# A fused backward pass of attention and FFN: when row layouts are staged, how many buffers two tiles have, and where the attention output is copied

## The chip, the cores and the metric

The kernel runs on one core of a Trainium2 chip. The core has a matmul engine (TensorE, PE in the profile; PEld is its weight load), VectorE (DVE), ScalarE (ACT), GpSimd (POOL) and SyncE (SP). Each takes its instructions in the order in which they were written. SP and POOL serve here mostly as queues that issue DMA transfers: an instruction that waits holds up everything behind it on that queue. The metric is the time of one execution on the device in microseconds.

## The reference

With x of 2048 rows of 448 numbers (16 heads of 28), the forward pass is a layer norm followed by an attention block and a gated FFN in parallel, and a residual:

```python
xn = layernorm(x)
q, k, v = split(xn @ wqkv)                  # 16 heads of 28
o = softmax(q @ k.T * 28 ** -0.5) @ v
out = x + o @ wo + (silu(xn @ w_gate) * (xn @ w_up)) @ w_down      # F = 1792
```

The kernel returns `out` and, for a given gradient of `out`, the gradients of x, wqkv, wo, w_gate, w_up and w_down: seven outputs in bf16.

## The kernel before

The work comes in four parts: a prologue (layer norm, transposed copies, the first group's projections), the forward loop, the backward loop over attention, and a last part that assembles the gradient of x. The change touches the forward loop alone.

The forward loop has 256 steps `(g, qc, kt)`: four groups `g` of four heads, four blocks `qc` of 512 queries, sixteen blocks `kt` of 128 keys. In a step PE makes the scores of four heads (L600) into two PSUM tiles `s_ps` of two heads each, of which there are two in all. ACT takes the exponential of each (L605) into a tile `eT`. PE then multiplies the exponentials of the step before with v (`pv`, L582) into the output tile `o_ps`, of which there is one. After the last key block, `pv` calls `o_items`: ACT copies `o_ps` to `o_raw` (L470), and two jobs are put in a queue: `tr`, four transposes of `o_raw` on PE (L479), and `do`, the projected gradient (L501). Their results are normalised on DVE, transposed by SP (L492, L523) and stored.

What is left of a step is filled with other matmuls by `fill(pace)`, which takes jobs from `queue` until the step's share of the remaining cost is used. `push(..., front=True)` puts jobs at the head; `behind=1` leaves the job that is first there in front of them. `cur` holds the rest of the job that is under way, and always comes first. The queue holds:

- the FFN, in 14 chunks `fc` of 128 columns and four row blocks `sc`. Each block makes three products in PSUM tiles `f_ps` (three in all, L383), from which DVE makes the three results in one tile `fT` (L407 and L417). SP transposes `fT` into `f_sp` (L419) and POOL stores it as three pieces of `hd_d` (L422).
- the weight gradients of the chunk before (L357), which need its `f_sp`: 16 matmuls for each of three weights, which take row blocks 0 to 3 in turn. The first weight's matmuls come in row block 1 of the next chunk.
- after a chunk, `weight_layout`: SP transposes a piece of a weight into the buffer `sp_stage` (L300), and POOL stores it (L302).
- at `qc == 2`, the next group's projections (L180), and `proj_done`, which stores them.
- `sp_layouts`, for the backward loop: it brings q and k of a group into row layout. SP transposes qT into `sp_stage` (L211), POOL stores it (L212), then the same for kT. There is one `sp_stage`, which `weight_layout` uses too. The job costs 0 in the planner and is pushed to the head of the queue at `kt == 0` of `qc == 1`. In that same step `pv` finishes block 0 of the queries, so `o_items` pushes its jobs behind the one job at the head, which then is `sp_layouts`.

Of the kernel before, what the change touches and what calls it, by code (L numbers as in the profile page):

```python
# [13 lines left out]
BF16 = mybir.dt.bfloat16  # L14
# [10 lines left out]
P = 128  # L25
NT = S // P
# [11 lines left out]
def kernel(  # L38
# [19 lines left out]
    pe, act, dve, pool, sp = nc.tensor, nc.scalar, nc.vector, nc.gpsimd, nc.sync  # L58
# [11 lines left out]
    spq_d = dram.tile([G, P, NT * P], BF16, name="spq_d")  # L70
    spk_d = dram.tile([G, P, NT * P], BF16, name="spk_d")
# [25 lines left out]
    bst = ExitStack()  # L97
# [6 lines left out]
    wq_sb = w_buf[:].rearrange("p a b -> p (a b)")[:, :4 * 3 * G * P].rearrange(  # L104
        "p (c t g r) -> p c t g r", c=4, t=3, g=G)
    stg = bst.enter_context(tc.tile_pool(name="stg", bufs=1))
    ep = bst.enter_context(tc.tile_pool(name="ep", bufs=7))
    ps_s = bst.enter_context(tc.tile_pool(name="ps_s", bufs=2, space=PSUM))
    ps_o = bst.enter_context(tc.tile_pool(name="ps_o", bufs=1, space=PSUM))
    ps_f = bst.enter_context(tc.tile_pool(name="ps_f", bufs=3, space=PSUM))  # L110
# [17 lines left out]
    for b in (2, 3):  # L128
# [10 lines left out]
        out=r_ones[:], in_=ident_f[:].rearrange("p (a b) -> p a b", b=HP)[:, :, 28:30],  # L139
# [29 lines left out]
    qk_tiles = {}  # L169
# [35 lines left out]
        pool.dma_start(out=qT_d[g], in_=qT[:])  # L205
        pool.dma_start(out=kT_d[g], in_=kT[:])

    def sp_layouts(g):
        for tq, dst in ((0, spq_d), (1, spk_d)):
            s_ = stg.tile([P, NT, P], BF16, name="sp_stage")  # L210
            sp.dma_start_transpose(out=s_[:], in_=qk_tiles[(g, tq)][:])  # L211
            pool.dma_start(out=dst[g], in_=s_[:].rearrange("p t c -> p (t c)"))  # L212

    def ln_stats(b):
        for t in range(4 * b, 4 * b + 4):
# [71 lines left out]

    fst = ExitStack()
    ftmp = fst.enter_context(tc.tile_pool(name="ftmp", bufs=2))
    fT = fst.enter_context(tc.tile_pool(name="fT", bufs=3))  # L290
    spp = fst.enter_context(tc.tile_pool(name="spp", bufs=2))
    op_ = fst.enter_context(tc.tile_pool(name="op_", bufs=1))
    def weight_layout(c, i):
# [15 lines left out]
    def fill(budget):  # L309

        while budget > 0.05:
            if not cur:
                if not queue:
                    return
                cur.extend(queue.popleft())
            cost, fn = cur.popleft()
            fn()
            budget -= cost
            left[0] -= cost

    def push(jobs, front=False, behind=0):
        left[0] += sum(c for job in jobs for c, _ in job)
        if front:
            first = [queue.popleft() for _ in range(min(behind, len(queue)))]
            queue.extendleft(reversed(first + jobs))
        else:
            queue.extend(jobs)

    def proj_items(g):
        out = []  # L330
        for tq in range(3):
            for sc in range(4):
                box = {}

                def go(c, tq=tq, sc=sc, box=box):
                    if c == 0:
                        box["m"] = proj_unit(g, tq, sc, "dve")
                    box["m"](c)
                out.append([(MM, lambda c=c, go=go: go(c)) for c in range(4)])
        out.append([(0.0, lambda: proj_done(g))])  # L340
        return out
# [204 lines left out]
    def load_pair(pr, parts):  # L546

        g, r = pr // 2, 64 * (pr % 2)
        q = qkp.tile([P, S], BF16, name="qT")
        k = qkp.tile([P, S], BF16, name="kT")  # L550
        qd[pr] = (q, k)
        n = S // parts
        return [lambda i=i, dst=dst, r0=r0, src=src: sp.dma_start(
                    out=dst[r0:r0 + 64, i:i + n], in_=src[g, r:r + 64, i:i + n])
                for r0, srcs in ((0, (qT_d, kT_d)), (64, (dOT_d, vT_d)))
                for dst, src in zip((q, k), srcs) for i in range(0, S, n)]

    def load_group(g, parts, kpool):

        spt[g] = [qkp.tile([P, NT, P], BF16, name="v_sp"), kpool.tile([P, S], BF16, name="vT"),  # L560
                  qkp.tile([P, NT, P], BF16, name="O_sp")]
        spt[g][1] = spt[g][1][:].rearrange("p (t c) -> p t c", c=P)
        n = NT // parts
        return [lambda i=i, t=t, src=src: sp.dma_start(
                    out=t[:, i:i + n, :].rearrange("p t c -> p (t c)"), in_=src[g, :, i * P:(i + n) * P])
                for t, src in zip(spt[g], (spq_d, spk_d, spo_d)) for i in range(0, NT, n)]
# [8 lines left out]
    def pv(i):  # L575
        g, qc, kt = steps[i]
        if kt == 0:
            o_cur["o"] = ps_o.tile([P, 512], FP32, name="o_ps")
        o_ps, v = o_cur["o"], v_tiles[g]
        e = eTs.pop(i)  # L580
        for hh in range(4):
            pe.matmul(o_ps[HP * hh:HP * (hh + 1), :], lhsT=v[:, kt, HP * hh:HP * (hh + 1)],  # L582
                      rhs=e[hh // 2][:, hh % 2, :], start=(kt == 0), stop=(kt == NT - 1),
                      tile_position=(0, HP * hh), skip_group_check=True)
        if kt == NT - 1:
            o_items(g, qc, o_ps)

    for i, (g, qc, kt) in enumerate(steps):
        if kt == 0 and qc == 1:
            push([[(0.0, lambda g=g: sp_layouts(g))]], front=True)  # L590
        if kt == 0 and qc == 2 and g + 1 < G:
            push(proj_items(g + 1), front=True)
        qT, kT = qk_tiles[(g, 0)], qk_tiles[(g, 1)]
        pace = left[0] / (nst - i)
        eTs[i] = []
        pair = [ps_s.tile([P, 2, 512], FP32, name="s_ps") for _ in range(2)]
        for half, s_ps in enumerate(pair):
            for j in range(2):
                r = HP * (2 * half + j)
                pe.matmul(s_ps[:, j, :], lhsT=kT[r:r + HP, kt * P:(kt + 1) * P],  # L600
                          rhs=qT[r:r + HP, qc * 512:(qc + 1) * 512],
                          start=True, stop=True, tile_position=(r, 0))
        for s_ps in pair:
            e = ep.tile([P, 2, 512], BF16, name="eT")
            act.activation(out=e[:], in_=s_ps[:], func=ACT.Exp, scale=SCALE)  # L605
            eTs[i].append(e)
        if i >= 1:
            pv(i - 1)
        if g == G - 1 and qc == 2:
            if kt == 0:  # L610
                first = load_pair(0, 1) + load_group(0, 1, vp)
            elif kt % 2 and first:
                first.pop(0)()
        if i in (6, 8, 10, 12):
            j = i // 2 - 3
            sp.dma_start_transpose(out=woT[:, :, j * P:(j + 1) * P], in_=wo_pad[:, j, :])
        pv_next[0] = i
        fill(pace)
# [212 lines left out]
    for k in range(N + 2 * UW):  # L831
        W, pos = k // UW, k % UW
        if k < N:
# [16 lines left out]
            s_ps = ps_sd.tile([P, 2, 512], FP32, name="sd")  # L850
# [25 lines left out]
        if 1 <= k <= N:  # L876
# [5 lines left out]
            if qi not in TQ:  # L882
                sp.dma_start_transpose(out=dsT[:, :, :, qi * P:(qi + 1) * P].rearrange("p j c q -> p (j c) q"),
                                       in_=DS[k - 1][:].rearrange("p j c -> p (j c)"))
# [128 lines left out]
```

## Time and profile before

| | us |
|---|---|
| median of 3 runs (1550.44 to 1550.81) | 1550.76 |
| the profiled execution | 1549.43 |
| its span, first to last instruction | 1547.7 |
| forward loop, about 30 to 656 | 626 |
| backward loop, about 656 to 1490 | 834 |
| last part, from 1490 | 58 |

The mean granted clock of PE over the profiled execution is 0.978 of full speed.

A row of the order of time gives start, duration, engine, line, operation, and in brackets how long the engine stood idle before it and what ended that. "SPq" and "POOLq" are the engines' DMA queues; the duration of a DMA row is the time that issuing took, not that to its landing. A row of the waits gives the sum, the number and the longest. Since busy time is an average over parts with different limits, a change in the forward loop is read from that loop's rows.

### The profile page before, as it was taken

To read this page: it belongs to the slowest core of one execution; us is meant where nothing else is said; L and a number is where in the kernel's file an instruction comes from. 1 tells how busy PE (TensorE), PEld (TensorE's weight loads), DVE (VectorE), ACT (ScalarE), POOL (GpSimd) and SP (SyncE) were. 2 spreads that over 40 slices of the span, in tenths; PEclk is the share of its full clock that TensorE was granted. 3 is DMA by queue.
4 is the path that set the end of the run, shared out by engine and by line. 5 is a ranking of instruction groups with operands and counts; after the bars stand their busy time and mean duration, and the time that the engine had idled before them with its cause. 6 is when DMAs were issued, how large, how long until landed. Compare 5 with 4: busy or idle time off the path is not lost.

```text
span 1547.7 us, 32024 instructions
## 1 busy us (share of the span) xinstructions
PE 1412.8 (91%) x12176; PEld 597.7 (39%) x12176; DVE 1099.4 (71%) x1421; ACT 1187.9 (77%) x1333; POOL 396.1 (26%) x664
## 2 busy tenths in 40 slices
PE   6899999999999989988988988989999889999987
PEld 3333333333333333433433444433335333543353
DVE  7654555656666657476877877878878789888935
ACT  6898988888788878676767867878778778888724
POOL 4341433343435355310110111111102101111033
PEclk9999999999999999999999999999999999999999
DMA  9985758767978689799999999999999999999994
GB/s 225 189 174 113 157 101 173 161 142 141 179 154 164 148 173 215 159 205 200 214 204 206 196 199 205 198 200 198 207 197 197 200 192 197 174 192 215 188 274 142
DMA packets 682106, 285.12 MB, mean 184 GB/s; under 512 B 637136, under 2 KB 650464, under 8 KB 681952
## 3 DMA queue, kind: packets, MB, share of 16 engines
q1 hardware_dynamic: 652016, 210.03, 74.6%
q0 software_dynamic: 25968, 64.53, 16.8%
q10 hardware_dynamic: 3968, 8.52, 1.6%
q8 instruction: 95, 1.56, 0.4%
q14 instruction: 59, 0.48, 0.1%
HBM read 67.34 MB, written 63.44 MB: 85 GB/s over the span
## 4 chain that ended last, share of the span: by engine, by line
PE 56%; DMA 13%; ACT 13%; DVE 8%; issue 6%; SPq 1%; POOL 1%; ACTq 0%; DVEq 0%; POOLq 0%
DMA dsT<-ds 9%; PE f_ps L357 7%; PE sd L852 6%; PE s_ps L600 6%; PE f_ps L383 6%; ACT E L870 5%; PE aux L719 4%; PE acc L749 4%; PE aux L796 4%; PE aux L776 4%; PE o_ps L582 4%; ACT eT L605 4%; DVE ds L881 3%; ACT dsT L783 3%; PE aux L713 3%
## 5 line engine op out<-in xcount | busy, mean ns | idle before, releaser
L881 DVE TENSOR_TENSOR ds<-sd,E 128x1024 bf16<-128x1024 f32 x512 | 611.4, 1220 | 137.5 <-DMA dsT<-ds 52.6
L870 ACT ACTIVATE E<-sd 128x1024 bf16<-128x1024 f32 x512 | 516.9, 1024 | 178.4 <-PE sd L863 140.2
L605 ACT ACTIVATE eT<-s_ps 128x1024 bf16<-128x1024 f32 x512 | 495.8, 1026 | 93.1 <-PE s_ps L600 89.6
L852 PE MATMUL sd<-kT,qT 32*128 32x512 bf16 x1024 | 201.8, 390 | 24.7 <-DVE ds L881 22.3
L863 PE MATMUL sd<-kT,qT 32*128 32x512 bf16 x1024 | 202.6, 389 | 23.6 <-ACT E L870 22.7
L749 PE MATMUL acc<-ds,v_sp 128*32 128x512 bf16 x1024 | 204.6, 395 | 0.7 <-DVE ds L881 0.7
L749 PE MATMUL acc<-E,O_sp 128*32 128x512 bf16 x1024 | 204.3, 395 | 0.2 <-ACT dkv_o L755 0.2
L600 PE MATMUL s_ps<-qT,kT 32*128 32x512 bf16 x1024 | 148.0, 386 | 7.8 <-ACT eT L605 5.6
L422 POOL DMA_DIRECT2D hd_d<-fT x168 | 126.9, 769 | 15.5 <-DVE fT L407 6.8
L383 PE MATMUL f_ps<-xnT,wgu 128*128 128x512 bf16 x448 | 118.8, 383 | 4.9 <-DVE w_sb L409 4.7
L764 POOL DMA_DIRECT2D dqkv_d<-dkv_o x64 | 39.3, 619 | 289.1 <-ACT dkv_o L755 287.3
L719 PE MATMUL aux<-W,ck 128*128 128x448 bf16 x448 | 108.4, 359 | 3.4
L852 PEld LDWEIGHTS <-qT 32*128 32x128 bf16 x1024 | 51.3, 91 | 154.1 <-issue 145.5
L582 PE MATMUL o_ps<-eT,v_sp 128*32 128x512 bf16 x1024 | 103.4, 394 | 0.6
L357 PE MATMUL f_ps<-xn_sp,f_sp 128*128 128x448 bf16 x448 | 99.1, 354 | 0.0
L749 PEld LDWEIGHTS <-O_sp 128*32 128x32 bf16 x1024 | 50.4, 94 | 113.4 <-issue 103.4
L600 PEld LDWEIGHTS <-kT 32*128 32x128 bf16 x1024 | 40.7, 91 | 137.7 <-issue 132.7
L776 PE MATMUL aux<-ident_bf,ds 128*128 128x128 bf16 x1024 | 79.4, 221 | 11.2 <-DVE dq_acc L808 5.8
L863 PEld LDWEIGHTS <-qT 32*128 32x128 bf16 x1024 | 65.4, 91 | 62.1 <-issue 58.2
L357 PEld LDWEIGHTS <-f_sp 128*128 128x128 bf16 x672 | 58.2, 98 | 77.4 <-issue 23.4
L776 PEld LDWEIGHTS <-ds 128*128 128x128 bf16 x1024 | 61.8, 98 | 39.8 <-issue 39.4
L395 DVE SCALAR_TENSOR_TENSOR g<-t_sb,f_ps 128x512 f32<-128x512 f32 x56 | 38.4, 686 | 53.3 <-ACT t_sb L393 53.2
(133 smaller groups left out, 1766.5 us busy)
## 6 DMA issues: line engine op xcount, KB each, us to landing
hd_d<-fT POOLq DMA_DIRECT2D x168, 128.0 KB, 4.4
ck<-hd_d SPq DMA_DIRECT2D x32, 448.0 KB, 4.4
ck<-hd_d SPq DMA_DIRECT2D x16, 576.0 KB, 5.1
dsT<-ds SPq DMA_TRANSPOSE x384, 4.2
dqkv_d<-dkv_o POOLq DMA_DIRECT2D x64, 64.0 KB, 3.8
dq_c<-dqkv_d ACTq DMA_DIRECT2D x5, 768.0 KB, 6.5
W<-wT_d SPq DMA_DIRECT2D x14, 224.0 KB, 3.6
out_dram<-dw_o POOLq DMA_DIRECT2D x28, 96.0 KB, 4.0
```

What stands on the lines that cost most here:

```text
L357: pe.matmul(acc[:, :D], lhsT=src[:, 12 * (t // 4) + 4 * wi + t % 4, :], rhs=rhs[:, t, :D], start=(t == 0), stop=(t == NT - 1))
L383: pe.matmul(st[name][:], lhsT=w(c), rhs=src[:, tsl, c, :], start=(c == 0), stop=(c == 3))
L582: pe.matmul(o_ps[HP * hh:HP * (hh + 1), :], lhsT=v[:, kt, HP * hh:HP * (hh + 1)], rhs=e[hh // 2][:, hh % 2, :], start=(kt == 0), stop=(kt ...
L600: pe.matmul(s_ps[:, j, :], lhsT=kT[r:r + HP, kt * P:(kt + 1) * P], rhs=qT[r:r + HP, qc * 512:(qc + 1) * 512], start=True, stop=True, tile_ ...
L605: act.activation(out=e[:], in_=s_ps[:], func=ACT.Exp, scale=SCALE)
L719: return [lambda n=n: pe.matmul(ps[:, :D], lhsT=t[:, n, :], rhs=w[:, n, :], start=(n == 0), stop=(n == NFC - 1)) for n in range(NFC)]
L749: pe.matmul(acc[r:r + HP, :], lhsT=src[:, qt, 64 * hp + HP * j:64 * hp + HP * j + HP], rhs=m[:, j, :], start=(qt == 0), stop=(qt == NT - 1 ...
L776: pe.transpose(ps[:, i, :], ds[:, i // 4, (i % 4) * P:(i % 4 + 1) * P], ident_bf[:])
L852: pe.matmul(s_ps[:, j, :], lhsT=q[HP * j:HP * j + HP, qt * P:(qt + 1) * P], rhs=kv[HP * j:HP * j + HP, kc * 512:(kc + 1) * 512], start=Tru ...
L863: pe.matmul(d_ps[:, j, :], lhsT=q[r:r + HP, qt * P:(qt + 1) * P], rhs=kv[r:r + HP, kc * 512:(kc + 1) * 512], start=True, stop=True, tile_p ...
L870: act.activation(out=E[k][:], in_=s_ps[:], func=ACT.Exp, scale=SCALE)
L881: dve.tensor_tensor(out=DS[k - 1][:], in0=d_ps[:], in1=E[k - 1][:], op=ALU.mult)
```

## The change

Four edits:

1. `sp_layouts(g)`, which staged q and k one behind the other, becomes `sp_layout(g, tq)`, which stages one of them. q is staged in block 1 of the queries and k in block 2, each at `kt == 4` where both were at `kt == 0` of block 1. Both go to the head of the queue, as before.
2. `fT` has 4 buffers in place of 3.
3. `eT` has 5 buffers in place of 7.
4. `pv(i - 1)` is called after the first of a step's two exponentials, not after the second. PE's order within the step stays; what moves is the copy of `o_ps` to `o_raw` on ACT, which now stands between the two exponentials.

With `sp_layouts` gone from `kt == 0`, the job left in front of `tr` and `do` in block 1 is a job of the FFN, as it is in the other blocks (or one of the next group's projections). All other instructions are the same in number and kind; fillers move by a few places in the forward loop, and the backward loop's order is unchanged.

```diff
-    ep = bst.enter_context(tc.tile_pool(name="ep", bufs=7))
+    ep = bst.enter_context(tc.tile_pool(name="ep", bufs=5))
...
-    def sp_layouts(g):
-        for tq, dst in ((0, spq_d), (1, spk_d)):
-            s_ = stg.tile([P, NT, P], BF16, name="sp_stage")
-            sp.dma_start_transpose(out=s_[:], in_=qk_tiles[(g, tq)][:])
-            pool.dma_start(out=dst[g], in_=s_[:].rearrange("p t c -> p (t c)"))
+    def sp_layout(g, tq):
+        s_ = stg.tile([P, NT, P], BF16, name="sp_stage")
+        sp.dma_start_transpose(out=s_[:], in_=qk_tiles[(g, tq)][:])
+        pool.dma_start(out=(spq_d, spk_d)[tq][g], in_=s_[:].rearrange("p t c -> p (t c)"))
...
-    fT = fst.enter_context(tc.tile_pool(name="fT", bufs=3))
+    fT = fst.enter_context(tc.tile_pool(name="fT", bufs=4))
...
-        if kt == 0 and qc == 1:
-            push([[(0.0, lambda g=g: sp_layouts(g))]], front=True)
+        if kt == 4 and qc in (1, 2):
+            push([[(0.0, lambda g=g, qc=qc: sp_layout(g, qc - 1))]], front=True)
...
-        for s_ps in pair:
+        for half, s_ps in enumerate(pair):
             e = ep.tile([P, 2, 512], BF16, name="eT")
             act.activation(out=e[:], in_=s_ps[:], func=ACT.Exp, scale=SCALE)
             eTs[i].append(e)
-        if i >= 1:
-            pv(i - 1)
+            if half == 0 and i >= 1:
+                pv(i - 1)
```

## The prediction

> **What bounds the kernel now.** I read the page's head first, then busy time by stretch, then who waits for whom in the stretch that the change touches, then the order of time around the longest waits.
>
> ```profile
> span 1547.7 us, 32024 instructions
> ## 1 busy us (share of the span) xinstructions
> PE 1412.8 (91%) x12176; PEld 597.7 (39%) x12176; DVE 1099.4 (71%) x1421; ACT 1187.9 (77%) x1333; POOL 396.1 (26%) x664
> ```
>
> All edits lie in the forward loop of 256 steps, some 626 us long. Its stretch (length, then busy time of PE, PEld, DVE, ACT and POOL, then the granted clock):
>
> ```profile
> 30.00:656.00 626.00, 591.55 (x3924) 223.69 (x3923) 367.14 (x636) 527.45 (x584) 251.39 (x365) 0.98 0.79 160
> ```
>
> The matmul engine is the bound here: 591.55 of 626 us. ACT is second, with 527.45. So work that the change moves costs nothing in itself; what counts is PE's idle 34.5 us and the time that PE runs at a lower clock. The idle time, by who ended it (total, times, longest):
>
> ```profile
> PE f_ps L479 <- ACT o_raw L470: 8.8, 8, 1.8
> PE f_ps L357 <- DMA f_sp<-fT: 8.1, 2, 7.0
> PE s_ps L600 <- ACT eT L605: 5.6, 19, 0.5
> PE f_ps L383 <- DVE w_sb L409: 4.7, 5, 2.5
> PE f_ps L180 <- DVE w_sb L409: 2.2, 1, 2.2
> ```
>
> And four stretches of low clock, each right behind a wait of this list (the third number from the right is the granted clock):
>
> ```profile
> 70.00:76.00 6.00, 5.78 (x38) 3.06 (x39) 2.80 (x6) 3.21 (x5) 0.00 (x0) 0.50 0.98 145
> 216.00:219.00 3.00, 3.00 (x23) 1.87 (x24) 2.01 (x5) 1.04 (x2) 0.88 (x2) 0.51 1.30 96
> 404.00:407.00 3.00, 3.00 (x13) 0.64 (x12) 2.93 (x5) 0.68 (x1) 2.53 (x4) 0.50 1.31 154
> 546.00:550.00 4.00, 3.65 (x15) 1.06 (x16) 0.62 (x1) 1.71 (x2) 1.88 (x3) 0.50 1.01 232
> ```
>
> At half clock, half of PE's busy time is lost: 2.9, 1.5, 1.5 and 1.8 us.
>
> **Staging q and k apart (part A).** Before, both transposes go into one buffer, one behind the other, so k's waits until q has landed and been stored. Both stand on SP's queue ahead of everything else. The fourth group, in order of time:
>
> ```profile
> 525.71 1.72 SPq L211 DMA_TRANSPOSE sp_stage<-qT  x1
> 533.56 3.11 SPq L211 DMA_TRANSPOSE sp_stage<-kT  x1
> 536.77 1.22 SPq L492 DMA_TRANSPOSE oT<-O_sp  x1
> 539.31 0.36 SPq L494 DMA_DIRECT2D hd_d<-oT  x1
> 539.77 1.82 SPq L523 DMA_TRANSPOSE dOT<-dOl  x1
> 541.67 1.57 SPq L419 DMA_TRANSPOSE f_sp<-fT  x1
> ```
>
> The FFN result that the last row transposes was complete on DVE by 531.0 (second row below starts at 530.33 and takes 0.68). It left 10.7 us later, and PE stood until 546.35:
>
> ```profile
> 530.33 0.68 DVE L417 SCALAR_TENSOR_TENSOR fT<-f_ps,w_sb 128x512 bf16<-128x512 f32 x1
> ...
> 546.35 1.30 PE L357 MATMUL f_ps<-dy_sp,f_sp 128*128 128x448 bf16 x3 [7.05 <-DMA f_sp<-fT]
> ```
>
> After the change, in the order of SP's queue, this transpose (that of the last of a chunk's four query blocks, the one that PE needs soonest) stands ahead of the output's transpose, and q's staging comes one FFN block later. It could leave at 531 and land about 4.8 us later (the median row in the last fence), at 536; PE asked for it at 539.3 (546.35 less 7.05). So the wait goes whole, with its dip: 7.05 + 1.8 = 8.85 us. The transposes and the stores, four of each for q and for k, stay in number and size. POOL's stores wait as before for the transpose, but never for two in a row.
>
> What is late next? Each of the eight stagings can still find the buffer taken, by a weight layout, and hold SP meanwhile. The queue's waits of before show the prices:
>
> ```profile
> SPq L211 <- DMA spq_d<-sp_stage: 14.7, 4, 4.3
> SPq L211 <- DMA sp_stage<-qT: 10.1, 4, 2.9
> SPq L211 <- DMA wqT_d<-sp_stage: 9.1, 2, 4.7
> ```
>
> The first two rows, 6.2 us for each group, vanish. The third can come back: in the fourth group's new order a weight layout, 5.4 us in its store (last fence), stands ahead of q's staging with only three transposes between. Behind that staging waits the FFN transpose of the second query block, which PE wants only in the next chunk, about 40 us later (14 chunks in 626 us), and the fourth buffer below gives DVE room. By this the cost is nothing; at the other end it is a hit like the old one, 8.85. I take half a hit, 4.4, since one of eight stagings stands this way.
>
> **Four buffers of FFN results (part B).** With three, DVE waits until an old result has been stored:
>
> ```profile
> DVE fT L407 <- DMA hd_d<-fT: 10.4, 3, 6.2
> ```
>
> While it waits, the third FFN accumulator stays taken, and PE stops for it: the two longest waits on `w_sb` in the list, 2.5 and 2.2, follow the two long ones of DVE. With one buffer more, DVE waits for a store one query block older, and such blocks are some 11 us apart (626 us over 56), more than the 6.2. So 2.5 + 2.2 + 1.5 of dip = 6.2 us; nothing at the worst, if POOL's queue is what is late.
>
> **Five buffers of exponentials.** A step writes two, and the output matmuls of step i-1 stand ahead of the scores of step i+1 in PE's order, so no more than four are alive. Cost nothing; if PE fell behind, ACT would have no scores to work on either.
>
> **The output's transposes in the second query block (part C).** Before, the staging job sat at the head of the queue of fillers and took the place of the one job that should lie between the copy of the output and its transposes. PE ran into the copy:
>
> ```profile
> 70.22 1.12 PE L479 MATMUL f_ps<-ident_f,o_raw 128*128 128x128 f32 x4 [1.75 <-ACT o_raw L470]
> ...
> 215.88 1.01 PE L479 MATMUL f_ps<-ident_f,o_raw 128*128 128x128 f32 x4 [1.76 <-ACT o_raw L470]
> ...
> 524.78 0.66 PE L479 MATMUL f_ps<-ident_f,o_raw 128*128 128x128 f32 x4 [1.05 <-ACT o_raw L470]
> ...
> 651.14 0.66 PE L479 MATMUL f_ps<-ident_f,o_raw 128*128 128x128 f32 x4 [0.68 <-ACT o_raw L470]
> ```
>
> The staging now enters at the fifth step of a block, so an FFN job of four matmuls or more lies between. The first three waits go, with the dips at 70 and 216: 1.75 + 1.76 + 1.05 + 2.9 + 1.5 = 9.0 us. The last one, behind the loop, stays.
>
> The row of low clock stands first: 0.50 begins behind waits of 1.75 and 1.76 us. The Trainium skill, "TensorE: Matmul & The Clock Gate", section "What's actually happening", says that the clock halves after an idle window of about 3.4 us. By that rule waits of 1.75 or 2.5 us would cause no dip, and 5.9 us of the sum would stay; that is the second rival.
>
> **The copy between two exponentials (part D).** The other four waits of the first row, 8.8 - 4.56 - 0.68 = 3.6 us, go too, for the copy ends one exponential (about 1 us) sooner. In exchange the second exponential ends a copy later, and PE's second pair of scores of the next step needs its place. Timing, from a block's end:
>
> ```profile
> 521.82 0.72 PE L600 MATMUL s_ps<-qT,kT 32*128 32x512 bf16 x4
> 522.15 0.09 PEld L600 LDWEIGHTS <-kT 32*128 32x128 bf16 x1 [0.23 <-issue]
> 522.31 1.94 ACT L605 ACTIVATE eT<-s_ps 128x1024 bf16<-128x1024 f32 x2 [0.21 <-PE s_ps L600]
> ...
> 524.14 0.59 ACT L470 COPY o_raw<-o_ps 128x512 f32<-128x512 f32 x1
> ```
>
> Exponentials start 0.49 us after the step's scores; with the copy between, the second ends at 0.49 + 1.94 + 0.59 = 3.0. A step takes 626 / 256 = 2.45 us, less the stalls about 2.4, and its second pair of scores is due 0.33 later, at 2.7. So PE waits 0.3 us, 15 times: 4.5. Bounds: nothing, if a long filler covers it, and a whole exponential, 0.97, each time (14.6). ACT itself does not wait for the output matmuls: they run during the first exponential. Net: 4.5 - 3.6 = 0.9 lost.
>
> ```profile
> wT_d<-sp_stage POOLq DMA_DIRECT2D x6, 448.0 KB, 5.4
> f_sp<-fT SPq DMA_TRANSPOSE x56, 4.8
> ```
>
> **Sum.** -8.85 - 6.2 - 9.0 + 0.9 + 4.4 = -18.7 us. The profiled execution took 1549.43 us, of which 1547.7 are the span; that is 1.3 below the median of the runs, 1550.76. So 1530.7 by the profile, 1532 as a median. The backward loop keeps its order of instructions and starts earlier.
>
> **The rivals.** First: the fourth FFN buffer does not do what it says. If POOL stores late because it stands behind waits for transposes, DVE merely waits one block later. For it: the stores share POOL's queue with every wait named above; against it: only three of 56 results waited. 6.2 us stay: 1538.
>
> Second: the dips do not hang on the short waits. Against it, a dip follows 1.75 and 1.76; for it, no dip follows the 2.2. Then 2.9 + 1.5 + 1.5 stay, and only the 7 us wait's dip goes: 1538. The Trainium skill's rule on the clock gate, above, would lead here.
>
> Third: the copy delays PE by a whole exponential, so 0.97 and not 0.3 for each of 15: 10 us more, 1542. For it, ACT is busy 84% of the loop; against it, waits of PE on exponentials were 0.5 at most.
>
> Fourth, the other side: a staging that finds its buffer taken by a weight layout's store holds back the FFN transpose that PE needs next, at 8.85 us each. There are now eight such places, not four. Parts A to D give 23; from three such hits on (26.6) the kernel is slower, 1554 with three. For it, the two waits of 4.7 and less on `wqT_d`; against it, in the new queue order each staging lies behind the last block's transpose, or long ahead of it.
>
> **How the numbers follow.** Forecast 0.50 (1525 to 1541 on its own), first rival 0.10, second 0.10, third 0.13, fourth 0.13, and 0.04 that losses of several kinds eat the gain. About 0.2%, 3.1 us, can be told from no change. Faster: 0.50 + 0.10 + 0.10 + 0.11 of the third; slower: the fourth and 0.01; same: the rest. The low end is all gains without costs, 8.85 + 6.2 + 9.0 + 3.6 = 27.7 below: 1523. The high end, 1549, leaves out the fourth rival.
>
> **What would show it.** In the profile after: no wait of 7 us for `f_sp`; the staging's wait for its own store gone from SP's queue; DVE no longer waiting for `hd_d`; PE's wait for `o_raw` at about 1 us in total and that for the exponentials up by some 4; no half clock at 70 and 216; the loop near 607 us. I am wrong if a new long wait for `f_sp` stands behind a staging, or if the dips move to other places.

## The result, and the profile after

The changed kernel takes 1534.68 us (median of 5 runs, 1531.74 to 1537.83) against 1550.44 of the kernel before in the same comparison: a ratio of 0.9897, with a 95% interval of 0.9878 to 0.9915. Forecast were 1532 and a range of 1523 to 1549. Line numbers of the changed kernel are one lower from L210 on; in the experiments `a_stage` and `a_split` number their lines like it, `u_stage`, `a_exp`, `a_late`, `a_ffn` and `a_copy` like the kernel before.

The profiled execution of the changed kernel took 1534.68 us. Its head, and then the first matmul of the backward loop by its line (the number ahead of "to" is the start of the first, so the end of the forward loop; in the kernel before it is 656.4):

```profile
span 1532.9 us, 32019 instructions
```
```profile
L851 PE MATMUL sd<-kT,qT x1024: 371/385/605, 643.3 to 1453.2; 32*128 32x512 bf16 x171
```

So 13.1 of the 14.8 us of difference between the two spans lie in the forward loop; the rest takes 891.3 us before and 889.6 after. Who ended PE's waits in the loop after the change:

```profile
PE f_ps L356 <- DMA f_sp<-fT: 8.8, 3, 5.0
PE s_ps L599 <- ACT eT L604: 7.9, 26, 0.6
PE f_ps L382 <- DVE w_sb L408: 1.5, 2, 1.2
...
PE f_ps L478 <- ACT o_raw L469: 0.7, 1, 0.7
```

Two rows shrank: the wait for the output's copy from 8.8 to 0.7 us, and that for `w_sb` from 6.9 to 1.5. The row for exponentials rose by 2.3. The row for `f_sp` did not shrink at all. The 7 us wait of the fourth group is gone, as SP's queue there shows in order of time:

```profile
516.49 1.42 SPq L418 DMA_TRANSPOSE f_sp<-fT  x1
517.99 1.56 SPq L491 DMA_TRANSPOSE oT<-O_sp  x1
523.18 0.36 SPq L493 DMA_DIRECT2D hd_d<-oT  x1
523.64 1.76 SPq L522 DMA_TRANSPOSE dOT<-dOl  x1
525.49 1.26 SPq L299 DMA_TRANSPOSE sp_stage<-in_B_w_gate_dram  x1
526.84 1.21 SPq L163 DMA_TRANSPOSE wdT<-in_B_w_down_dram  x1
528.13 1.18 SPq L164 DMA_TRANSPOSE wdT<-wd  x1
529.41 1.46 SPq L418 DMA_TRANSPOSE f_sp<-fT  x1
534.64 3.65 SPq L210 DMA_TRANSPOSE sp_stage<-qT  x1
538.34 1.55 SPq L418 DMA_TRANSPOSE f_sp<-fT  x1
```

The urgent FFN transpose (first row) now leaves ahead of the output's, and q's staging follows the weight layout with three transposes between. But two other waits for `f_sp` grew: 3.65 us near 70 us, where 1.05 stood before, and a new one of 5.0 us in the last chunk. Each has its half clock (behind the stretch stand its length and PE's busy time; the third number from the right is the granted clock):

```profile
70.00:73.00 3.00, 3.00 (x15) 0.75 (x13) 0.43 (x1) 1.78 (x3) 0.00 (x0) 0.56 0.85 164
622.00:629.00 7.00, 4.16 (x16) 1.23 (x17) 0.62 (x1) 1.94 (x2) 3.46 (x5) 0.51 1.01 228
```

The new wait in the last chunk, SP's queue and then PE:

```profile
602.36 3.65 SPq L491 DMA_TRANSPOSE oT<-O_sp  x1
611.40 0.37 SPq L493 DMA_DIRECT2D hd_d<-oT  x1
611.88 1.19 SPq L522 DMA_TRANSPOSE dOT<-dOl  x1
613.16 1.45 SPq L418 DMA_TRANSPOSE f_sp<-fT  x1
614.78 1.49 SPq L368 DMA_TRANSPOSE dw_o<-dwT  x1
616.36 3.89 SPq L418 DMA_TRANSPOSE f_sp<-fT  x1
```
```profile
624.84 1.30 PE L356 MATMUL f_ps<-dy_sp,f_sp 128*128 128x448 bf16 x3 [5.00 <-DMA f_sp<-fT]
```

SP stood from 606.0 to 611.4, until the output's transpose had landed and could be stored, with the FFN's transposes behind it. That is part of the delay. DVE had completed the result of the last row of SP's queue by 613.57:

```profile
612.89 0.68 DVE L416 SCALAR_TENSOR_TENSOR fT<-f_ps,w_sb 128x512 bf16<-128x512 f32 x1
```

So its transpose was 2.8 us late on SP's queue (616.36), and then took 8.4 us to land, where the median is 4.9.

### The profile page after: what moved, and what is told of

It is laid out like the page before. It is cut to its first block, busy times and chain, and to the rows that moved or that the text cites. A ratio compares the mean times of both kernels' runs of the same rounds, so it can differ in the third digit from the quotient of the medians.

```text
span 1532.9 us, 32019 instructions
## 1 busy us (share of the span) xinstructions
PE 1414.2 (92%) x12176; PEld 600.1 (39%) x12176; DVE 1100.7 (72%) x1421; ACT 1187.9 (77%) x1333; POOL 395.0 (26%) x664
## 4 chain that ended last, share of the span: by engine, by line
PE 59%; ACT 13%; DMA 12%; DVE 8%; issue 6%; POOL 1%; SPq 0%; DVEq 0%; ACTq 0%; POOLq 0%
DMA dsT<-ds 9%; PE f_ps L356 8%; PE s_ps L599 7%; PE f_ps L382 7%; PE sd L851 6%; ACT E L869 5%; PE aux L718 5%; PE acc L748 4%; PE o_ps L581 4%; ACT eT L604 4%; PE aux L775 4%; DVE ds L880 4%; PE aux L795 3%; ACT dsT L782 3%; PE f_ps L180 3%
## 5 line engine op out<-in xcount | busy, mean ns | idle before, releaser
L862 PE MATMUL sd<-kT,qT 32*128 32x512 bf16 x1024 | 203.4, 390 | 22.2 <-ACT E L869 21.3
L599 PE MATMUL s_ps<-qT,kT 32*128 32x512 bf16 x1024 | 152.8, 383 | 10.1 <-ACT eT L604 7.9
```

The source lines that it names most:

```text
L862: pe.matmul(d_ps[:, j, :], lhsT=q[r:r + HP, qt * P:(qt + 1) * P], rhs=kv[r:r + HP, kc * 512:(kc + 1) * 512], start=True, stop=True, tile_p ...
```

## The experiments

The table gives, for each kernel, the median of its runs, the ratio to the kernel before with its interval, and from the profiled execution: the end of the forward loop, PE's idle time in it from 30 us on, and PE's time lost to a reduced clock there (worked out over stretches of 1 us: busy time of PE times one less the granted clock). `after_again` is the changed kernel once more, beside `u_ffn2`, `v_store` and `a_copy`. The rows come from four comparisons, each with its own runs of the kernel before (medians 1548.12 to 1550.44), so the ratios compare across rows, and the medians only roughly.

| kernel | median us | ratio (95%) | loop end | PE idle | lost to clock |
|---|---|---|---|---|---|
| before | 1550.44 | | 656.4 | 34.9 | 8.3 |
| after | 1534.68 | 0.9897 (0.9878-0.9915) | 643.3 | 23.0 | 3.5 |
| after_again | 1532.29 | 0.9884 (0.9851-0.9917) | 644.2 | 22.6 | 4.6 |
| u_stage | 1541.60 | 0.9944 (0.9922-0.9966) | 652.1 | 30.6 | 4.5 |
| u_ffn | 1528.17 | 0.9856 (0.9812-0.9900) | 642.8 | 21.2 | 4.8 |
| u_ffn2 | 1531.22 | 0.9876 (0.9842-0.9911) | 639.5 | 21.3 | 2.3 |
| u_copy | 1535.15 | 0.9901 (0.9871-0.9931) | 642.2 | 23.1 | 2.0 |
| a_exp | 1551.73 | 1.0010 (0.9986-1.0033) | 660.7 | 36.7 | 9.9 |
| a_stage | 1538.11 | 0.9912 (0.9883-0.9941) | 645.9 | 25.6 | 5.6 |
| a_split | 1538.35 | 0.9916 (0.9886-0.9946) | 647.9 | 28.5 | 6.6 |
| a_late | 1537.98 | 0.9925 (0.9891-0.9959) | 646.9 | 28.5 | 4.3 |
| a_ffn | 1544.67 | 0.9955 (0.9932-0.9979) | 651.4 | 32.4 | 4.5 |
| a_copy | 1550.97 | 1.0003 (0.9981-1.0025) | 652.7 | 31.0 | 4.6 |
| v_store | 1526.96 | 0.9842 (0.9807-0.9877) | 633.7 | 16.7 | 0.0 |

Single executions of one kernel differ by several us, in the loop and outside it: `a_exp`, which should move nothing, ends its loop 4.3 us later than the kernel before in the profiled execution while its runs show no change. The profiled execution was the slowest of its kernel for `u_stage`, `u_ffn`, `a_exp` and `v_store`. So, by this one pair, ends of loops tell apart what differs by more than some 4 us; below that only the rows of the waits do. Nor do the last two columns add up to the loop: from the kernel before to the changed one they fall by 16.7 us together and the loop by 13.1. What makes up the rest is not shown.

`after_again` was expected to have a wait for `f_sp` of 3 us or more near 70 and of 4 to 6 us near 625. It has 5.64 us near 625, and near 70 two waits of 1.19 and 1.93.

**u_stage: the staging undone.**

```diff
...
-        if kt == 4 and qc in (1, 2):
-            push([[(0.0, lambda g=g, qc=qc: sp_layout(g, qc - 1))]], front=True)
+        if kt == 0 and qc == 1:
+            push([[(0.0, lambda g=g: sp_layouts(g))]], front=True)
```

> The changed kernel with q and k again staged one behind the other at the start of block 1. My terms: the wait for the FFN transpose near the fourth group's staging comes back (7 us and its half clock, together near 9), and PE runs into the output's copy again in block 1; since the copy now stands between the exponentials these waits are up to 1 us shorter each, so 3 to 9 us with their dips. Less the half hit that I had charged: 1543 to 1549. Rival: the gain came from how the fillers happened to fall, and the staging's place matters little: 1532 to 1538.

It took 1541.6, some 7 us more than the changed kernel and just below what my terms had. The long wait is back in its old place, in SP's queue and on PE:

```profile
518.42 2.68 SPq L211 DMA_TRANSPOSE sp_stage<-qT  x1
529.45 1.99 SPq L211 DMA_TRANSPOSE sp_stage<-kT  x1
...
536.84 2.47 SPq L419 DMA_TRANSPOSE f_sp<-fT  x1
```
```profile
541.62 1.30 PE L357 MATMUL f_ps<-dy_sp,f_sp 128*128 128x448 bf16 x3 [9.90 <-DMA f_sp<-fT]
```

The waits for the copy of the output, though, rose only to 2.8 us, and no half clock followed them: with the early copy, part C was worth little more.

**u_ffn and u_ffn2: three buffers of FFN results in the changed kernel**, run in two comparisons.

```diff
-    fT = fst.enter_context(tc.tile_pool(name="fT", bufs=4))
+    fT = fst.enter_context(tc.tile_pool(name="fT", bufs=3))
```

> The changed kernel with three buffers of FFN results. My term: DVE waits for stores of hd_d again, some 10 us in all, PE waits 4 to 5 us more for w_sb, and the time is 4 to 7 us longer: 1539 to 1542. Rival: with the staging apart, POOL's queue is early enough for three buffers; no wait of DVE for hd_d, and 1533 to 1537.

> The changed kernel with three buffers of FFN results again, for an interval against the changed kernel. If the fourth buffer is worth nothing once the staging is moved: within 3 us of the changed kernel, DVE waiting for hd_d some 5 us and PE for w_sb some 8 us, where the changed kernel waits as long for f_sp. My term B, 6 us for the buffer, would have it at 1538 to 1542.

Neither is slower than the changed kernel: 1531.2 beside 1532.3 in the same comparison, with intervals that overlap nearly whole, and 1528.2 in the other. My term of 6 us fell. The rival's reason fell too: DVE does wait for stores again, and PE for DVE. Waits of DVE, then of PE, in `u_ffn2`:

```profile
DVE fT L406 <- DMA hd_d<-fT: 6.0, 1, 6.0
```
```profile
PE s_ps L599 <- ACT eT L604: 8.7, 26, 0.8
PE f_ps L382 <- DVE w_sb L408: 8.2, 3, 6.4
...
PE f_ps L356 <- DMA f_sp<-fT: 0.6, 1, 0.6
```

The wait changed its place: with three buffers PE stands 6.4 us for `w_sb` near 591 us, and then finds the last chunk's transposes landed; with four it runs on and stands 5 us for `f_sp` near 625.

**a_ffn: four buffers and the five of exponentials, alone on the kernel before.**

> The kernel before with four buffers of FFN results and five of exponentials, nothing else. My term B: no wait of DVE for stores of hd_d, PE's waits for w_sb fall from 7 us to about 2, 1543 to 1546. Rival, seen when the fourth buffer was taken from the changed kernel: the waits move to other transposes and nothing is gained, 1548 to 1552.

Alone it gains: 1544.7, ratio 0.9955, and DVE no longer waits for `hd_d` at all. PE's waits in it:

```profile
PE f_ps L357 <- DMA f_sp<-fT: 10.0, 3, 6.7
...
PE f_ps L383 <- DVE w_sb L409: 1.8, 4, 0.8
```

The `w_sb` waits fell from 6.9 to 1.8 us, as part B had it, and the 6.7 us wait for `f_sp` at the fourth staging stayed.

**u_copy and a_copy: the copy moved behind both exponentials in the changed kernel, and moved between them alone on the kernel before.**

```diff
-            if half == 0 and i >= 1:
-                pv(i - 1)
+        if i >= 1:
+            pv(i - 1)
```

> The changed kernel with the copy of the attention output behind both exponentials again. My terms: PE waits 3 to 4 us more for the copy and 2 to 4 us less for exponentials, so no change that can be measured: 1532 to 1537. Rival: the early copy was a gain of its own, since the second exponential has slack: 3 to 5 us longer, 1538 to 1540.

> The kernel before with the copy of the attention output between the two exponentials and nothing else. My term D and what it does in block 1: PE's wait for the copy falls from 8.2 to 2 to 4 us, its wait for exponentials rises by 3 to 4 us; the half clock near 216 goes with the shorter wait. 1546 to 1550. Rival: PE waits a whole exponential at every copy, 8 to 14 us more: 1555 to 1562.

Neither run can be told from its base: a ratio of 0.9901 where the changed kernel has 0.9897, and one of 1.0003. Both waits moved the forecast way. Without the early copy in the changed kernel PE waits 2.5 us for `o_raw` and 4.5 for exponentials, with it 0.7 and 7.9. On the kernel before the copy's wait fell from 8.8 us to 3.4, as expected, and that for exponentials rose by 0.8, where 3 to 4 were expected. PE's waits there with the early copy:

```profile
PE f_ps L357 <- DMA f_sp<-fT: 7.7, 2, 6.9
PE s_ps L600 <- ACT eT L605: 6.4, 20, 0.5
PE f_ps L383 <- DVE w_sb L409: 4.1, 5, 1.8
PE f_ps L479 <- ACT o_raw L470: 3.4, 6, 0.8
```

The half clock near 70 and 216 is absent there, but one near 251 is new, and the time does not show a gain.

**a_exp: five buffers of exponentials, alone.**

> The kernel before with five buffers of exponentials and nothing else. My term: no change, 1549 to 1552, and no wait of ACT on the output matmuls. Rival: ACT is held by buffers now and then and the loop grows by several us.

A ratio of 1.0010 whose interval holds 1: no change, as forecast. What the edit does is make room: by their shapes in the kernel, two tiles of exponentials less free 4 KB of each partition, and one tile of FFN results more takes 3. That a fourth FFN buffer would not fit beside seven is not shown by a run here.

**a_stage, a_split, a_late: the first edit alone on the kernel before, and its two halves.** `a_stage` stages each at the fifth step of its block. `a_split` has them in different blocks but at the first step; `a_late` has both in block 1, one behind the other, at the fifth step:

```diff
-        if kt == 0 and qc == 1:
+        if kt == 4 and qc == 1:
             push([[(0.0, lambda g=g: sp_layouts(g))]], front=True)
```

> The kernel before with the first edit alone: q staged in block 1 and k in block 2, each at the fifth step. If the staging's move carries the change: the 7 us wait for an FFN transpose near the fourth group's staging is gone, PE's waits for the copy of the output fall from 8.2 to about 4 us, the half clock behind them goes, and 10 to 15 us are gained: 1535 to 1541 against 1550. Rival: the gain needs the fourth FFN buffer as well, since DVE still waits for stores of hd_d at some 250 and 400 us: 1542 to 1546.

> The kernel before with q and k staged in different blocks, but each at the first step of its block, where both stood: split without delay. If it is the wait between the two stagings that costs (SP held from q's store to k's transpose): the 7 us wait is gone or below 2 us, the waits for the output's copy stay at 8 us with their half clock, and 1539 to 1543. Rival: what costs is that the staging stands ahead of the output's transposes and of the FFN transpose behind them, split or not: a wait of 3 us or more for f_sp stays at some block's start, 1545 to 1552.

> The kernel before with q and k staged one behind the other as before, but four steps later, at the fifth step of block 1: delay without split. If it is the wait between the two stagings that costs, a long wait for f_sp stays somewhere, 5 us or more, and only the waits for the output's copy in block 1 go (4.6 us and 4 us of half clock): 1541 to 1545. Rival, the place in SP's queue is what counts, since the urgent FFN transpose has left by then: no wait for f_sp over 2 us beside the one near 67 us, 1533 to 1540.

All three take 1538, some 12 us less than before. So the first edit alone has some four fifths of the whole gain, and either half of it has nearly all of that. The rest is not clear of the noise: the interval of `a_stage`, 0.9883 to 0.9941, holds the 0.9897 of the changed kernel, so no run shows that the other three edits add anything to the first.

In `a_stage` the waits for the copy fell to 2.5 us and the longest for `f_sp` to 2.5, as expected; a wait of 4.8 us for `w_sb` near 593 stands in the list instead, since DVE with its three buffers still waits for `hd_d` (8.3 us in all). Each half takes the long wait out in its own way. The longest waits of PE in `a_split`:

```profile
PE f_ps L478 <- ACT o_raw L469: 9.7, 8, 1.8
PE s_ps L599 <- ACT eT L604: 6.0, 22, 0.5
PE f_ps L356 <- DMA f_sp<-fT: 3.4, 1, 3.4
```

and in `a_late`, where SP still waits between q and k, as long as before (the last fence is that of SP's queue):

```profile
PE f_ps L383 <- DVE w_sb L409: 9.5, 5, 7.4
PE s_ps L600 <- ACT eT L605: 5.8, 23, 0.5
PE f_ps L501 <- DVE w_sb L409: 4.6, 1, 4.6
```
```profile
PE f_ps L357 <- DMA f_sp<-fT: 0.2, 1, 0.2
```
```profile
SPq L211 <- DMA spq_d<-sp_stage: 14.6, 4, 4.2
SPq L211 <- DMA sp_stage<-qT: 9.0, 4, 2.6
```

In `a_late` the held queue does no harm to `f_sp`, because the urgent transpose has left; the waits for buffers of FFN results grew instead, to 7.4 and 4.6 us. I had expected one of the two to be the cause and the other to be worth little. In `a_split` the signs of the first theory came (no 7 us wait, though one of 3.4 near 325 is left; the copy's waits as before), in `a_late` those of its rival. Both theories for `a_split` and `a_late` are answered in the same way: a held queue costs where an urgent transpose stands behind it, and that takes both the hold and the place.

**v_store: one thing more, from the last chunk's wait.** SP issues the store of `oT` behind the next transpose, so that it does not stand waiting for the landing of the first:

```diff
-            sp.dma_start(out=hd_d[tsl, :, g, :].rearrange("k p s -> p k s"),
-                         in_=oT[:].rearrange("p (k s) -> p k s", k=4))
+            st["oT"] = oT
...
+            sp.dma_start(out=hd_d[tsl, :, g, :].rearrange("k p s -> p k s"),
+                         in_=st["oT"][:].rearrange("p (k s) -> p k s", k=4))
             pool.dma_start(out=dOT_d[g, :, qc * 512:(qc + 1) * 512], in_=dT[:])
```

> The changed kernel with one thing more: SP issues the store of the transposed output behind the next transpose, not in front of it, so that SP's queue does not wait for the landing of the first with FFN transposes behind it (9 us in the last chunk). If a held SP queue is still what costs: the 5 us wait for f_sp in the last chunk falls below 2 us with its half clock, the loop ends 4 to 8 us sooner, 1526 to 1531. Rival: the transfers themselves are slow there, so the transposes land as late as before: 1532 to 1537.

Its loop ends at 633.7 us, 10.5 before that of the changed kernel in the same comparison, with no stretch of reduced clock. PE's only wait for `f_sp`, and SP's waits ahead of that store (57 us in the changed kernel there, 25 here):

```profile
PE f_ps L356 <- DMA f_sp<-fT: 1.0, 1, 1.0
```
```profile
SPq L523 <- DMA oT<-O_sp: 25.0, 12, 4.0
```

The wait in the last chunk is gone, and so is most of the one near 70 us. In the last chunk the result is complete at 610.85, and its transpose leaves at once:

```profile
610.88 1.76 SPq L418 DMA_TRANSPOSE f_sp<-fT  x1
```

It lands 4.4 us later, against 8.4 in the changed kernel. So the rival, slow transfers, is not ruled out: both the time in the queue (2.8 us to nothing) and that of the transfer (8.4 to 4.4) fell, and no run takes the two apart. The median is 1526.96 against 1532.29, the lowest of all in that comparison, with intervals of the two ratios that still overlap; its profiled execution gave the 10 us back behind the loop (896.7 us there, 886.7 in the other), where the order of instructions is the same. PE's idle time grew there by 6 us and its time lost to the clock by 5; why is not shown. So a shorter loop is shown, and a faster kernel is not.

## Why the prediction was right, point by point

The forecast was -18.7 us; the medians say -15.8 and the profiled executions -14.8. The loop, where all of it should have come, has 13.1 of that: it takes 613 us where the text had 607. Direction and place were right, and the staging carries the gain. That the size came out as near as it did is in part luck. Some 2 us of it lie behind the loop, where nothing was changed; the 6.2 us of the FFN buffer did not come, and the 4.4 us held back for a hit of the staging were more than used up by waits of another origin.

Of the signs named, the wait of 7 us went, the staging no longer waits for its own store, DVE no longer waits for `hd_d`, and PE waits 0.7 us for `o_raw`. The wait for exponentials rose by 2.3 us, not by some 4. Half clock near 216 is gone, but near 70 it is not (0.56 from 70 to 73). And one of the two signs of being wrong came: a stretch of half clock stands near 622, where none stood before.

**Staging (A).** Right. The 7.05 us wait vanished for the reason given: the urgent transpose stands ahead of the output's, and undoing the edit brings back 9.90 us behind the same chain. The collision that I saw in the fourth group came as well (SP waits 3.7 us for `wT_d`, from 530.9 to 534.6 in the rows above) and cost nothing, as the text said of the transpose behind it.

**The half hit of 4.4 us.** Too small, and for another reason. No staging held an urgent transpose, so the fourth rival fell. But 7.7 us of waits for `f_sp` came elsewhere, with half clock behind them. The 5.0 us in the last chunk come behind another hold of SP's queue, the store of `oT`, which I had seen in the rows of SP and not followed to the last chunk; `v_store` shows that they go with it, though not how much of them was the hold and how much the slower transfer. Near 70 us no such store stands ahead of the wait in SP's queue. There its size goes, on the whole, with the fourth FFN buffer. SP's row for the same transpose, before and after:

```profile
55.18 1.44 SPq L419 DMA_TRANSPOSE f_sp<-fT  x1
```
```profile
55.39 4.17 SPq L418 DMA_TRANSPOSE f_sp<-fT  x1
```

In all eight profiles with three buffers this issue takes 1.44 to 1.46 us, and PE waits 0 to 2.3 us in all for `f_sp` up to 80 us; in all six with four it takes 2.7 to 4.3, and PE waits 1.0 to 3.8. Why the issue takes longer there stays open.

**Four FFN buffers (B).** Mis-sized. 6.2 us was the worth of the edit alone, and alone it gave 5.8. In the changed kernel its worth cannot be told from zero. The step that failed was to add it to the others: the waits that the buffer removes are handed on to the next transpose, unless that is on time. The first rival had this worth right, nothing, and the mechanism wrong: the buffer does what it says (no wait of DVE for `hd_d` in the changed kernel or in `a_ffn`), and it is PE's next wait, for `f_sp`, that takes the gain.

**The second block's transposes (C).** The waits of 4.56 us went. Of the 4.4 us of half clock the part near 216 went; near 70 a stretch half as long stayed, now behind the wait for `f_sp`. And nothing shows that the two belong to this part alone: `a_copy`, with the staging where it was, loses both dips, and `a_split`, with the waits as long as before, loses the one near 216. In the kernel before, the dip near 70 hung on two waits, that of 1.05 us for `f_sp` and that of 1.75 for the copy (see the last section).

**The copy (D).** 0.9 us of loss, measured as no change. The exchange is as described, of smaller size: with the early copy in the changed kernel PE waits 1.8 us less for the copy and 3.4 us more for exponentials, where the text had 3.6 and 4.5. The third rival, a whole exponential at each copy, fell: 0.6 us at most.

## What to carry to other kernels

On a queue that issues in order, ask of each wait what stands behind it and by when it is needed; a transfer without a deadline can be moved behind the urgent one, or split, and either was enough here. Gains from two edits that work on one chain of buffers are not to be added: take the second away from the changed kernel before it is credited. A wait that is removed shows up next at the following link, so look for the next hold of the same queue, here a store that waited for a landing. A stretch of half clock is not a fixed price of the wait ahead of it, so a sum that counts it should say that it may come or not.

## What the runs showed of the hardware that I had not expected

Behind or within each of 20 waits of 2.5 to 9.9 us in the loops of these profiles lies a stretch at half clock, waits of 2.52 and 3.00 among them. The Trainium skill's "TensorE: Matmul & The Clock Gate", section "What's actually happening", has the matmul clock fall after an idle window of about 3.4 us. By these waits less is enough. Below 2.5 us it is not the length of the wait that decides: after 2.44 us in `u_copy` the clock stayed full, and after 1.76 us it fell in the kernel before and did not fall in `a_split`, where 1.60 us was enough later on:

```profile
214.48 0.66 PE L478 MATMUL f_ps<-ident_f,o_raw 128*128 128x128 f32 x4 [1.76 <-ACT o_raw L469]
...
560.52 0.66 PE L478 MATMUL f_ps<-ident_f,o_raw 128*128 128x128 f32 x4 [1.60 <-ACT o_raw L469]
```
```profile
214.00:218.00 4.00, 3.29 (x34) 1.87 (x34) 3.65 (x8) 2.65 (x4) 1.46 (x2) 1.00 1.19 146
560.00:565.00 5.00, 4.48 (x32) 2.67 (x32) 3.36 (x8) 2.40 (x3) 1.82 (x3) 0.66 1.02 203
```

The clock records of the fourteen traces show what decides for the most part. Within one execution every stretch at half clock begins on a grid of steps of 3.41 us (to within 3 ns), and in the forward loop it lasts one to four whole steps. Counted over the loops of all fourteen: of the steps at full clock, all 26 in which PE was idle for more than 52% were followed by a step at half clock, none of the 2415 below 34%, and 6 of the 25 between. After a step at half clock the next was at half clock again in all 20 cases where PE had been idle for more than 15% of it, and at full clock in all 32 where it had been idle for less than 13%. So a wait counts for less if two steps share it: of the 2.44 us in `u_copy`, 1.0 lie in one step and 1.4 in the next. And short waits add up if they fall into one step: the one ahead of the dip near 70 in the kernel before holds 0.9 us of the wait for `f_sp` and 0.8 of that for the copy. The grid does not lie at one place of the kernel: half clock begins at 69.22 us in `after` and at 71.01 in `after_again`, which are the same kernel.

So the second rival is answered for the most part: the dips hang on the waits, but on how much of one step these fill. Whether a wait of 1.5 to 2.5 us costs a dip is then partly chance, and I should not have counted the dips near 70 and 216 as certain.
